# Raw down weights in two buffers loaded a unit ahead, and two steps of the operand and weight preparation moved

## The chip, the cores and the metric

The kernel runs on one core of a Trainium2 chip. The time is the device time of one execution in microseconds, as a median over runs. A core has TensorE (PE, matrix products), VectorE (DVE), ScalarE (ACT), GpSimd (POOL) and SyncE (SP, which here only issues DMAs); PEld is TensorE's loading of weights.

## The reference

Two branches on the same 2048 x 576 input are mixed by a gate. The second branch, a gated network with 4608 hidden columns, takes most of the time.

```python
x = A_x                                          # 1 x 2048 x 576, float32
g = _sigmoid((x * gate_w).sum(-1, keepdims=True))
a = _A_ref(x, A_wqkv, A_w_phi, A_wo)             # linear attention, 32 heads, learned feature map
b = _B_ref(x, B_W_gate, B_W_up, B_W_down)
return g * a + (1 - g) * b

def _B_ref(x, W_gate, W_up, W_down):             # 576 x 4608, 576 x 4608, 4608 x 576
    gate = jnp.einsum("bsd,df->bsf", x, W_gate)
    up = jnp.einsum("bsd,df->bsf", x, W_up)
    gate = gate * (lambda x, dt: x.astype(dt))(gate > 0, gate.dtype)
    h = gate * up
    return jnp.einsum("bsf,fd->bsd", h, W_down)
```

## The kernel before

**Arithmetic.** Each float32 operand is split into a high and a low part (`high` on ScalarE, `low` on VectorE), and a product is the sum of high x high, low x high and high x low on TensorE. Products of 2 x 2 blocks are made with seven block products in place of eight, from sums and differences of blocks (of the input `xo`, of the gate and up weights `wb`/`ws`, of the down weights `wd`).

**Order of the work.** The attention branch fills the first 340 us or so. Then come 72 *units*: units 0 to 35 do the first half of the rows for each of 36 blocks of hidden columns, units 36 to 71 the second half. A unit is seven *steps* j = 0 to 6, all written by `step(u, j)`; each engine works through its instructions in the order in which they are written (`in_order`). A step has one block product of the gate/up stage on PE (`product`, line 1140, seven matmuls; the seven operands are taken in the order `SEQ` = 1, 5, 6, 2, 7, 3, 4) and one block product of the down stage (`down`, line 1171, three matmuls, and two more for the rest columns in some steps). The down stage works on pairs of units: in an odd unit it does the second half (m = 1) of the pair before, in an even unit the first (m = 0) of the pair just made. So two units hold 14 x 7 + 14 x 3 + 8 = 148 matmuls: 78 in an even unit and 70 in an odd one.

**Down weights.** `load_down(g)` brings the raw down weights of pair g, `wdr`, 128 x 1152, into a single buffer, at step 5 of an even unit (line 918). `prepare_down` makes the operands `wd` from them in the next odd unit (m = 0) and the even one after it (m = 1): step 0 high parts of three blocks (ACT, line 1103), step 1 their low parts (DVE, 1106), step 2 four sums of blocks on GpSimd, in place in `wdr` (1092 to 1095), step 4 the high and step 5 the low parts of these. The rest columns go with m = 0 (`rest_weights`).

**At the turn**, units 35 to 37, the seven operands of the second half replace those of the first, as `swap_in` writes it: operands 1 and 5 come through `xr` (high part, line 827, and low part with its rest rows, 831 and 841), the others are loaded into `xo` and split in place (856, 857, 861), with the rest rows' low part on GpSimd (841).

**In the first half** VectorE and ScalarE also make the operands `wb` and `ws` of the unit to come, from raw weights `wr`, and store them to memory (`wbd`, `wsd`); the second half only loads these (911, 912).

**Copies that PE needs.** In step 1 ScalarE copies `cx` to `cy` (line 1379); the product of step 2 writes `cx` again. In step 5 VectorE adds `cx` into `u` (1383) before the product of step 6.

Of the kernel before, what the change touches and what calls it, by code (L numbers as in the profile page):

```python
# [7 lines left out]
F32 = mybir.dt.float32  # L8
# [7 lines left out]
P = 128  # L16
# [67 lines left out]
def gated_mix_kernel(  # L84
# [24 lines left out]
    nc = tc.nc  # L109
# [101 lines left out]
    with tc.tile_pool(name="ps_v", bufs=1, space=PSUM) as ps_v:  # L211
# [7 lines left out]
        for k in range(5):  # L219
            w = raw.tile([P, TB + VW], F32, name="xwv", tag="raw")  # L220
# [559 lines left out]
    wdrp = ctx.enter_context(tc.tile_pool(name="wdrp", bufs=1, **L_))  # L780
# [54 lines left out]
    def operand(hf, i):  # L835
        operand_high(hf, i)
        operand_low(hf, i)
# [26 lines left out]
    RAW, WO, WDR = {}, {}, {}  # L864
    units = [(0, c) for c in range(NC)] + [(1, (c - 2) % NC) for c in range(NC)]
# [46 lines left out]
        nc.sync.dma_start(o.bitcast(F32), wsd[c])  # L912
        WO[u] = {1: (b, 0), 2: (b, 1), 4: (b, 2), 5: (o, 2), 6: (o, 0), 7: (o, 3), 3: (o, 1)}

    def load_down(g):
        if g < 2 * NG:
            WDR[g] = wdrp.tile([P, 9 * P], F32, name="wdr")
            nc.sync.dma_start(WDR[g], wd[units[2 * g][1] // 2])

    def low_parts(f, u):  # L920
        f(u, low_w)
# [79 lines left out]
    with in_order(tc, nc, nc.tensor, nc.vector, nc.scalar, nc.gpsimd, nc.sync):  # L1001
        project_out(2, 1)
        for k in (2, 1, 0):
            quotient(3, k)
        for k in (2, 1, 0):
            operand_rows(3, k)
        whole(x1)
        RS.close()
        pad = ctx.enter_context(tc.tile_pool(name="pad2", bufs=1, **R_))
        pad.tile([P, 24], F32, name="pad2")  # L1010
        xo2 = ctx.enter_context(tc.tile_pool(name="xo2", bufs=4, **R_))
        wop = ctx.enter_context(tc.tile_pool(name="wop", bufs=2, **R_))
        wraw = ctx.enter_context(tc.tile_pool(name="wraw", bufs=2, **R_))
        load_w(0)
        load_w(1)
        for i in range(3, 7):
            load_in_place(0, i)
        load_rests(0, (3, 4, 5))
        load_down(0)
        project_out(2, 2)  # L1020
        blocks(0, high_w)
        low_parts(blocks, 0)
        project_out(2, 3)
        project_out(2, 4)
        blocks(1, high_w)
        sums_of_blocks(0)
        operand_high(0, 2)
        project_out(3, 0)
        block_sums(0, high_w)
        low_parts(blocks, 1)  # L1030
        operand_low(0, 2)
        load_rests(0, (6,))
        load_w(2)
        low_parts(block_sums, 0)
        high_in_place(0, 3)
        project_out(3, 1)
        low_of_place(3)
        sums_of_blocks(1)
        high_in_place(0, 4)
        project_out(3, 2)  # L1040
        high_in_place(0, 5)
        low_of_place(4)
        project_out(3, 3)
        block_sums(1, high_w)
        low_parts(block_sums, 1)
        low_of_place(5)
        project_out(3, 4)
# [18 lines left out]
    WD, W4, HID, ACC, ACC4, BANK, REST = {}, {}, {}, {}, {}, {}, {}  # L1066
# [6 lines left out]


    def down_raw(g, m):
        return WDR[g][:, m * 4 * P:(m + 1) * 4 * P].rearrange("p (b q) -> p b q", b=4)

    def down_tile():
        return wdp.tile([P, 18 * P], F32R, name="wd")
# [27 lines left out]

    def rest_weights(g, step):

        a = WDR[g][:, 8 * P:].rearrange("p (c q) -> p c q", c=2)  # L1110
        if step == 0:
            nc.scalar.activation(W4[g][:, 0:2, 0], a, AF.Copy)
        elif step == 1:
            tt(out=W4[g][:, 0:2, 1], in0=a, in1=W4[g][:, 0:2, 0].bitcast(F32), op=SUB)  # L1114
            pt(out=a[:, 0], in0=a[:, 0], in1=a[:, 1], op=ADD)  # L1115
        elif step == 2:
            nc.scalar.activation(W4[g][:, 2, 0], a[:, 0], AF.Copy)
            nc.scalar.activation(W4[g][:, 3], W4[g][:, 1].bitcast(F32), AF.Copy, scale=-1.0)
        else:
            tt(out=W4[g][:, 2, 1], in0=a[:, 0], in1=W4[g][:, 2, 0].bitcast(F32), op=SUB)  # L1120

    def plain_down(g, f):

        if f is high:
            o = down_tile()
            WD[g] = o[:, :16 * P].rearrange("p (s q) -> p s q", s=2)
            W4[g] = o[:, 16 * P:].rearrange("p (b s q) -> p b s q", b=2, s=2)
        f(WD[g], WDR[g][:, :8 * P])
        f(W4[g].rearrange("p b s q -> p s b q"), WDR[g][:, 8 * P:].rearrange("p (b q) -> p b q", b=2))

# [157 lines left out]
    def swap_in(u, j):  # L1290

        i = j + 7 * (u - NC + 1)
        if 2 <= i < 7:
            if i in (2, 3):
                load_rests(1, (2, 3, 4) if i == 2 else (5, 6))
            load_in_place(1, i)
        if i in (1, 2):
            operand(1, i - 1)
        if 2 <= i - 5 < 7:
            low_in_place(1, i - 5)  # L1300
        if 2 <= i - 4 < 7:
            high_in_place(1, i - 4)
        if 2 <= i - 5 < 7:
            low_rest(1, i - 5, pt)
# [48 lines left out]
    def prepare_down(g, m, j):  # L1353

        if j == 0:
            down_blocks(g, m, high)
        elif j == 1:
            down_blocks(g, m, low)
        elif j == 2:
            down_sums_of_blocks(g, m)  # L1360
        elif j == 4:
            down_block_sums(g, m, high)
        elif j == 5:
            down_block_sums(g, m, low)
        if m == 0 and j in (0, 1, 4, 5):
            rest_weights(g, (0, 1, 4, 5).index(j))

    def step(u, j):


        g, odd = divmod(u, 2)
        v, q = u + 1, g - 1
# [16 lines left out]
        old = not odd and g > 0  # L1389

        if j == 0:
            if u > 0:
                a = gate_last(*LATE.pop())
# [85 lines left out]
        elif j == 6:  # L1479
            a = T["g2"]  # L1480
# [5 lines left out]
            w = WO.pop(u)  # L1486
# [11 lines left out]
            prepare_down(g, 0, j)  # L1498
        elif old:
            prepare_down(q, 1, j)  # L1500
        if old and j == 5:
            load_down(g)
        if old and j == 6:
            ODD.pop(q)
        if g > 0:
            s = 7 * odd + j
# [35 lines left out]
    with in_order(tc, nc, nc.tensor, nc.vector, nc.scalar, nc.gpsimd, nc.sync):  # L1542
# [4 lines left out]
        g = 2 * NG - 1  # L1547
# [86 lines left out]
def _layout(A_x, A_wqkv, A_w_phi, A_wo, B_W_gate, B_W_up, B_W_down, gate_w):  # L1634
    import numpy as np

    xT = np.ascontiguousarray(_by_tiles(A_x[0].T).swapaxes(0, 1))
    xs = np.ascontiguousarray(_by_halves(A_x[0].T).transpose(2, 0, 1, 3))
    wqT = _by_groups(np.concatenate([A_wqkv[:, :D].T, A_wqkv[512:, :D].T], axis=1))
    wkT = _by_groups(np.concatenate([A_wqkv[:, D:2 * D].T, A_wqkv[512:, D:2 * D].T], axis=1))  # L1640
    v = np.zeros((D, VW), A_wqkv.dtype)
    v[:, 0] = gate_w
    for j in range(NQ):
        n = NV[j]
        v[:, j * GS + 1:j * GS + 1 + n] = A_wqkv[:, 2 * D + QG * j:2 * D + QG * j + n]
    wv = np.ascontiguousarray(_by_tiles(v).swapaxes(0, 1))
    phi = np.zeros((FG, NF, FG), A_w_phi.dtype)
    for h in range(H):
        j, i = divmod(h, FH)
        phi[i * DH:(i + 1) * DH, j, i * DH:(i + 1) * DH] = A_w_phi[h]  # L1650
    wo = np.concatenate([A_wo, A_wo[:, 512:]], axis=1)
    wo_rows = [r for k in range(4)
               for r in (*range(G * k, G * k + QG),
                         *range(4 * G + k // 2 * QG + k % 2 * 20, 4 * G + k // 2 * QG + k % 2 * 20 + 20),
                         *range(G * k + QG, G * k + G))]
    wo_rows += [*range(4 * G + 40, 4 * G + QG), *range(5 * G - 14, D)] * 2
    wo = np.ascontiguousarray(wo[wo_rows].reshape(5, P, 5, P).transpose(2, 1, 0, 3))
    g, u = (_by_halves(w).reshape(2, 3, P, NC, P) for w in (B_W_gate, B_W_up))
    wgu = np.stack([g[0], g[1], u[1], u[0]])
    wgu = np.ascontiguousarray(wgu.transpose(3, 2, 0, 1, 4))  # L1660
    d = B_W_down.reshape(NC // 2, 2, P, D)
    halves = d[..., :512].reshape(NC // 2, 2, P, 2, 2, P)
    blocks = [halves[:, 0, :, 0], halves[:, 1, :, 0], halves[:, 1, :, 1], halves[:, 0, :, 1]]
    blocks = np.stack(blocks, axis=2).transpose(0, 1, 3, 2, 4).reshape(NC // 2, P, 8 * P)
    wd = np.ascontiguousarray(np.concatenate([blocks, d[:, 0, :, 512:], d[:, 1, :, 512:]], axis=2))
    ident = np.eye(P, dtype=np.float32)
    mask = np.zeros((QK, QG + 4), np.float32)
    spread = np.zeros((4, H, 5, P), np.float32)
    copies = spread[:2]
    for r in range(QK):  # L1670
        h = r // (2 * DH)
        mask[r, h * DH:(h + 1) * DH] = 1.0
        mask[r, QG + h] = 1.0
        mask[r, QG + 3] = 1e-6 if r % (2 * DH) < DH else 0.0
    for k in range(5):
        for r in range(P):
            copies[:, wo_rows[k * P + r] // DH, k, r] = 1.0
    spread = spread.reshape(4 * H, 5, P)
    return {"xT": xT, "xs": xs, "wqT": wqT, "wkT": wkT, "wv": wv, "phi": phi, "wo": wo, "wgu": wgu,
            "wd": wd, "ident": ident, "mask": mask,  # L1680
            "spread": spread}
# [16 lines left out]
```

## Time and profile before

| | |
|---|---|
| runs | 1574.77, 1574.79, 1572.11 us; median 1574.77 |
| profiled execution | 1575.22 us, of it the span of the trace 1573.5 |
| PE busy | 1553.8 us, 99% of the span, 7715 matmuls |
| DVE, ACT, POOL busy | 1249.5 (79%), 800.8 (51%), 272.9 us (17%) |
| TensorE clock granted, mean | 0.998 |
| DMA | 283.43 MB, 180 GB/s in the mean |

PE's busy time is a modelled one: a matmul shows some 391 ns, while the next begins well before that has passed, so the pace is read from how many matmuls lie in a stretch. A few records of matmuls can be missing. A wait is shown as engine and line, the tile's name, and behind the arrow what came last. "SPq" is the queue in which SP issues DMAs. Idle time of an engine costs something only where PE comes to wait for it.

### The profile page before, as it was taken

Reading aid. Unit: us, or ns where it says so; the run is one execution under the profiler, and the core shown is the slowest. Engines: PE = TensorE matmul, PEld = TensorE weight load, DVE = VectorE, ACT = ScalarE, POOL = GpSimd, SP = SyncE. Lnnn points to the kernel's source line nnn. Section 1 sums busy time; section 2 is a strip of 40 time slices with the busy share of each in tenths; the row PEclk is TensorE's granted clock in tenths of the full one; section 3 lists DMA queues with packets and bytes.
Section 4 is the critical chain, followed back from the end, with each engine's and each line's share of the span. In section 5 each row is a group of like instructions: output and inputs, shape, how many; then the busy total and the mean of one; then the engine's idle time right before and its main releaser. Section 6 shows DMA issues by size and latency. Waiting matters only on the chain.

```text
span 1573.5 us, 20844 instructions
## 1 busy us (share of the span) xinstructions
PE 1553.8 (99%) x7715; PEld 1294.8 (82%) x7715; DVE 1249.5 (79%) x1964; ACT 800.8 (51%) x1408; POOL 272.9 (17%) x405
## 2 busy tenths in 40 slices
PE   9999999999999999999999998999999999999998
PEld 9999996687887888877888886888888888888886
DVE  4997776499999989998988988767667777667776
ACT  4354335566777767767777775332333332332332
POOL 0126522112111112111111113111111111111110
PEclk9999999999999999999999999999999999999999
DMA  5355405596755585565455424643443433433432
GB/s 165 105 197 188 174 27 150 184 359 270 265 200 201 216 286 206 217 224 212 175 214 224 187 96 161 223 153 137 182 152 132 181 141 147 186 138 135 188 133 75
DMA packets 64545, 283.43 MB, mean 180 GB/s; under 512 B 6802, under 2 KB 17298, under 8 KB 55740
## 3 DMA queue, kind: packets, MB, share of 16 engines
q1 hardware_dynamic: 61228, 270.34, 47.0%
q0 software_dynamic: 2352, 10.11, 1.9%
q10 hardware_dynamic: 864, 1.65, 0.3%
q8 instruction: 61, 1.00, 0.3%
q14 instruction: 40, 0.33, 0.1%
HBM read 172.07 MB, written 108.60 MB: 178 GB/s over the span
## 4 chain that ended last, share of the span: by engine, by line
PE 78%; DVE 15%; DMA 4%; ACT 1%; issue 1%; POOL 0%; SPq 0%; ACTq 0%; DVEq 0%; POOLq 0%
PE cx L1140 23%; PE pd L1171 16%; PE ca L1140 11%; PE cy L1140 6%; PE kv L175 4%; PE pk L175 3%; PE pq L175 3%; DMA wdr<-wd 3%; PE pm L1171 3%; DVE hl L1276 2%; DVE ac L1237 2%; DVE ws L877 1%; DVE g L1325 1%; PE kv L421 1%; DVE wd L1106 1%
## 5 line engine op out<-in xcount | busy, mean ns | idle before, releaser
L1171 PE MATMUL pd<-hh,wd 128*128 128x512 f32 x980 | 383.2, 391 | 0.1
L1186 DVE TENSOR_TENSOR ac<-pd,ac 128x512 f32<-128x512 f32 x238 | 164.5, 691 | 139.6 <-PE pd L1171 139.5
L1140 PE MATMUL cx<-xo,ws 128*128 128x512 f32 x1008 | 254.6, 392 | 10.0 <-ACT cy L1379 7.8
L1140 PE MATMUL cx<-xo,wb 128*128 128x512 f32 x1008 | 252.8, 391 | 0.7 <-DVE u L1383 0.7
L1140 PE MATMUL ca<-xo,ws 128*128 128x512 f32 x1008 | 252.8, 391 | 0.0
L1271 ACT ACTIVATE hh<-g 128x512 fp32r<-128x512 f32 x249 | 148.3, 623 | 201.0 <-DVE g L1325 183.6
L1140 PEld LDWEIGHTS cx<-xo,ws 128*128 128x128 f32 x1008 | 188.0, 188 | 54.9 <-ACT cy L1379 14.1
L1140 PEld LDWEIGHTS cx<-xo,wb 128*128 128x128 f32 x1008 | 188.6, 188 | 42.1 <-DVE u L1383 2.7
L1140 PEld LDWEIGHTS ca<-xo,ws 128*128 128x128 f32 x1008 | 189.9, 188 | 39.7 <-DVE xo L861 0.4
L1171 PEld LDWEIGHTS pd<-hh,wd 128*128 128x128 f32 x980 | 184.6, 188 | 39.2 <-ACT pd L1220 0.8
L1171 PE MATMUL pd<-hl,wd 128*128 128x512 f32 x490 | 191.6, 391 | 0.0
L1276 DVE TENSOR_TENSOR hl<-g,hh 128x512 fp32r<-128x512 f32 x249 | 173.0, 695 | 0.2 <-ACT hh L1271 0.2
L1103 ACT ACTIVATE wd<-wdr 128x384 fp32r<-128x384 f32 (+2 forms) x142 | 80.9, 570 | 161.7 <-DMA wdr<-wd 134.8
L1140 PE MATMUL cy<-xo,wb 128*128 128x512 f32 x504 | 126.7, 391 | 0.0
L1092 POOL TENSOR_TENSOR wdr<-wdr 128x128 f32<-128x128 f32 x70 | 33.5, 478 | 472.5 <-DVE wd L1106 472.5
L1140 PEld LDWEIGHTS cy<-xo,wb 128*128 128x128 f32 x504 | 95.3, 189 | 19.9
L1171 PEld LDWEIGHTS pd<-hl,wd 128*128 128x128 f32 x490 | 92.2, 188 | 19.7 <-DVE hl L1276 0.7
L1106 DVE TENSOR_TENSOR wd<-wdr,wd 128x384 fp32r<-128x384 f32 (+2 forms) x142 | 88.2, 622 | 23.7 <-ACT wd L1103 23.1
L1325 DVE TENSOR_TENSOR g<-g,g 128x512 f32<-128x512 f32 x140 | 97.5, 697 | 2.4
L1115 POOL TENSOR_TENSOR wdr<-wdr 128x64 f32<-128x64 f32 x35 | 11.5, 329 | 502.2 <-DVE wd L1114 493.4
L1237 DVE TENSOR_TENSOR ac<-pd,ac 128x512 f32<-128x512 f32 x114 | 78.1, 685 | 6.9 <-PE pd L1171 5.8
L1340 ACT ACTIVATE g<-cx 128x512 f32<-128x512 f32 x73 | 43.5, 596 | 78.5 <-PE cx L1140 77.5
(259 smaller groups left out, 2721.2 us busy)
## 6 DMA issues: line engine op xcount, KB each, us to landing
wsd<-ws SPq DMA_DIRECT2D x34, 1280.0 KB
ws<-wsd SPq DMA_DIRECT2D x34, 1280.0 KB
wbd<-wb SPq DMA_DIRECT2D x34, 960.0 KB
wb<-wbd SPq DMA_DIRECT2D x34, 960.0 KB
wr<-wgu SPq DMA_DIRECT2D x36, 768.0 KB
wdr<-wd SPq DMA_DIRECT2D x36, 576.0 KB
eT<-et SPq DMA_DIRECT2D x10, 594.0 KB
xt<-xb SPq DMA_DIRECT2D x7, 768.0 KB
```

The source lines that it names most:

```text
L175: nc.tensor.matmul(ps, w, m, start=i == 0, stop=i == len(pairs) - 1)
L1092: pt(out=a[:, 2], in0=a[:, 2], in1=a[:, 3], op=ADD)
L1103: nc.scalar.activation(o[:, 0], a, AF.Copy)
L1106: tt(out=o[:, 1], in0=a, in1=o[:, 0].bitcast(F32), op=SUB)
L1140: nc.tensor.matmul(ps, w, v, start=first and m == 0, stop=m == len(pairs) - 1, skip_group_check=True)
L1171: mm = lambda ps, w, v, a, z: nc.tensor.matmul(ps, w, v, start=a, stop=z, skip_group_check=True)
L1186: tt(out=a, in0=ps, in1=a, op=ADD)
L1237: tt(out=a, in0=ps, in1=a, op=ADD)
L1271: nc.scalar.activation(h, src, AF.Copy)
L1276: tt(out=l, in0=src, in1=h.bitcast(F32), op=SUB)
L1325: tt(out=b, in0=a, in1=b, op=SUB)
L1340: nc.scalar.activation(a, ps, AF.Copy)
```

## The change

It has three parts, and a layout that goes with them.

1. The raw down weights of a pair lie in two buffers, `wdr0` (128 x 640: the first four blocks and the rest columns) and `wdr1` (128 x 512: the other four). Part 0 is loaded at step 0 of an even unit and read from step 0 of the odd unit after it; part 1 is loaded at step 0 of an odd unit and read from step 0 of the next even one.
2. At the turn, operand 1's high part stays in step 1 of unit 35, and its low part goes to step 2; operand 5's high part goes to step 3 and its low part to step 4. Before, both parts were made in one step, 1 and 2.
3. GpSimd's sums of down weight blocks are written at step 3, not at step 2.

```diff
-    def load_down(g):
+    def load_down(g, m):
         if g < 2 * NG:
-            WDR[g] = wdrp.tile([P, 9 * P], F32, name="wdr")
-            nc.sync.dma_start(WDR[g], wd[units[2 * g][1] // 2])
+            n = 5 - m
+            w = WDR[g, m] = wdrp.tile([P, n * P], F32, name=f"wdr{m}")
+            nc.sync.dma_start(w, wd[units[2 * g][1] // 2, :, 5 * P * m:5 * P * m + n * P])
...
-        load_down(0)
+        load_down(0, 0)
+        load_down(0, 1)
...
     def down_raw(g, m):
-        return WDR[g][:, m * 4 * P:(m + 1) * 4 * P].rearrange("p (b q) -> p b q", b=4)
+        return WDR[g, m][:, :4 * P].rearrange("p (b q) -> p b q", b=4)
...
-        if i in (1, 2):
-            operand(1, i - 1)
+        if i in (2, 4):
+            operand_low(1, i // 2 - 1)
+        if i in (1, 3):
+            operand_high(1, i // 2)
...
-        elif j == 2:
+        elif j == 3:
             down_sums_of_blocks(g, m)
...
-        if old and j == 5:
-            load_down(g)
+        if old and j == 0:
+            load_down(g, 0)
+        if odd and j == 0 and g > 0:
+            load_down(g, 1)
```

`rest_weights` and `plain_down` read the same blocks from the two buffers (the last pair's high and low parts are made in two instructions in place of one), and the host lays the blocks out in the new order. The lines below 918 move down by one to seven.

How the instructions move is shown at three places.

*SP in the first half.* An even and an odd unit, before: `wr` are the raw gate and up weights for the unit after next, `wbd` and `wsd` the stores of steps 2 and 5.

```order
L870 DMA wr_6630<-wgu 128x1536
L1448 DMA wbd_68<-wb_6628 128x1920
L1456 DMA wsd_69<-ws_6708 128x2560
L918 DMA wdr_6749<-wd 128x1152
L328 DMA xt_66<-xb_5701 128x3x256
L870 DMA wr_6787<-wgu 128x1536
L1448 DMA wbd_68<-wb_6785 128x1920
```

And after, an odd and an even unit:

```order
L870 DMA wr_5893<-wgu 128x1536
L919 DMA wdr1_5898<-wd 128x512
L1453 DMA wbd_68<-wb_5891 128x1920
L1461 DMA wsd_69<-ws_5958 128x2560
L328 DMA xt_66<-xb_5715 128x3x256
L870 DMA wr_6041<-wgu 128x1536
L919 DMA wdr0_6045<-wd 128x640
L1453 DMA wbd_68<-wb_6039 128x1920
```

One load behind the stores of the even unit has become one in each unit, behind the load of `wr` and ahead of the stores.

*VectorE in unit 35.* `pd` is the down stage's sum, 831 and 841 are the low parts of operands 1 and 5. Before:

```order
L1114 TENSOR_TENSOR wd_8879<-wdr_8845,wd_8879 128x2x64
L831 TENSOR_TENSOR xo_8908<-xr_8710,xo_8908 128x1024
L841 TENSOR_TENSOR xo_8908<-xr_8710,xo_8908 32x512
L1237 TENSOR_TENSOR ac_3683<-pd0_8904,ac_3683 128x512
L831 TENSOR_TENSOR xo_8935<-xr_8712,xo_8935 128x1024
L841 TENSOR_TENSOR xo_8935<-xr_8712,xo_8935 32x512
L1276 TENSOR_TENSOR hl_8899<-g1_8824,hh_8898 128x512
```

After:

```order
L1116 TENSOR_TENSOR wd_8913<-wdr0_8766,wd_8913 128x2x64
L1240 TENSOR_TENSOR ac_3685<-pd0_8940,ac_3685 128x512
L831 TENSOR_TENSOR xo_8944<-xr_8744,xo_8944 128x1024
L841 TENSOR_TENSOR xo_8944<-xr_8744,xo_8944 32x512
L1279 TENSOR_TENSOR hl_8935<-g1_8860,hh_8934 128x512
L1330 TENSOR_TENSOR g1_8860<-g2_8830,g1_8860 128x512
L1240 TENSOR_TENSOR ac_3683<-pd0_8940,ac_3683 128x512
L831 TENSOR_TENSOR xo_8991<-xr_8746,xo_8991 128x1024
```

The addition of `pd` now stands ahead of operand 1's low part, and three instructions between that and operand 5's.

*GpSimd in unit 36, and SP behind it.* The rest rows of operands 6, 2, 7, 3 and 4 (841) and the four sums, before:

```order
L841 TENSOR_TENSOR xo_8933<-xr_8929,xo_8933 32x512
L841 TENSOR_TENSOR xo_8957<-xr_8929,xo_8957 32x512
L1092 TENSOR_TENSOR wdr_8845<-wdr_8845 128x128
L1093 TENSOR_TENSOR wdr_8845<-wdr_8845 128x128
L1094 TENSOR_TENSOR wdr_8845<-wdr_8845 128x128
L1095 TENSOR_TENSOR wdr_8845<-wdr_8845 128x128
L841 TENSOR_TENSOR xo_8981<-xr_8929,xo_8981 32x512
L841 TENSOR_TENSOR xo_8998<-xr_8954,xo_8998 32x512
```

After:

```order
L841 TENSOR_TENSOR xo_8963<-xr_8959,xo_8963 32x512
L841 TENSOR_TENSOR xo_8989<-xr_8959,xo_8989 32x512
L841 TENSOR_TENSOR xo_9015<-xr_8959,xo_9015 32x512
L1094 TENSOR_TENSOR wdr1_8916<-wdr1_8916 128x128
L1095 TENSOR_TENSOR wdr1_8916<-wdr1_8916 128x128
L1096 TENSOR_TENSOR wdr1_8916<-wdr1_8916 128x128
L1097 TENSOR_TENSOR wdr1_8916<-wdr1_8916 128x128
L841 TENSOR_TENSOR xo_9034<-xr_8986,xo_9034 32x512
```

Operand 7's rest rows now come before the sums. SP in the same units, the load for unit 37 first before and then after:

```order
L1247 DMA outT<-ac_3682 128x512
L918 DMA wdr_9155<-wd 128x1152
L1247 DMA outT<-ac_3680 128x512
L1148 DMA ac_3680<-att_64 128x512
L1247 DMA outT<-ac_3682 128x512
```
```order
L846 DMA xo_9052<-xt_66 128x1024
L919 DMA wdr0_9072<-wd 128x640
L1250 DMA outT<-ac_3682 128x512
L1250 DMA outT<-ac_3684 128x512
L1250 DMA outT<-ac_3682 128x512
```

The load has moved from between the stores of the outputs to just behind the last operand's load.

More of the change, by code (lines that the diff above doesn't have):

```diff
@@ L1108, in rest_weights @@
     def rest_weights(g, step):
-        a = WDR[g][:, 8 * P:].rearrange("p (c q) -> p c q", c=2)
+        a = WDR[g, 0][:, 4 * P:].rearrange("p (c q) -> p c q", c=2)
         if step == 0:
@@ L1127, in plain_down @@
             W4[g] = o[:, 16 * P:].rearrange("p (b s q) -> p b s q", b=2, s=2)
-        f(WD[g], WDR[g][:, :8 * P])
-        f(W4[g].rearrange("p b s q -> p s b q"), WDR[g][:, 8 * P:].rearrange("p (b q) -> p b q", b=2))
+        for m in range(2):
+            f(WD[g][:, :, 4 * P * m:4 * P * (m + 1)], WDR[g, m][:, :4 * P])
+        f(W4[g].rearrange("p b s q -> p s b q"), WDR[g, 0][:, 4 * P:].rearrange("p (b q) -> p b q", b=2))
     def product(ps, u, n, first):
@@ L1664, in _layout @@
     blocks = np.stack(blocks, axis=2).transpose(0, 1, 3, 2, 4).reshape(NC // 2, P, 8 * P)
-    wd = np.ascontiguousarray(np.concatenate([blocks, d[:, 0, :, 512:], d[:, 1, :, 512:]], axis=2))
+    wd = np.ascontiguousarray(np.concatenate([blocks[:, :, :4 * P], d[:, 0, :, 512:], d[:, 1, :, 512:], blocks[:, :, 4 * P:]], axis=2))
     ident = np.eye(P, dtype=np.float32)
```

## The prediction

> **What bounds the kernel now.** I read the engine totals first, then busy time by stretches, then who waited for whom, then the order of time at the few places where TensorE stood.
>
> ```profile
> PE 1553.8 (99%) x7715; PEld 1294.8 (82%) x7715; DVE 1249.5 (79%) x1964; ACT 800.8 (51%) x1408; POOL 272.9 (17%) x405
> ```
> ```profile
> core 0: us, PE busy (x) PEld busy (x) DVE busy (x) ACT busy (x) POOL busy (x), PEclk, DMA share, GB/s
> 600.00:650.00 50.00, 50.00 (x221) 41.05 (x220) 47.89 (x75) 37.52 (x64) 8.09 (x13) 1.00 0.53 200
> 650.00:700.00 50.00, 48.52 (x212) 39.19 (x212) 45.08 (x69) 34.95 (x61) 8.11 (x14) 1.00 0.63 233
> 1000.00:1050.00 50.00, 50.00 (x223) 41.42 (x222) 34.14 (x58) 16.27 (x33) 6.51 (x14) 1.00 0.43 162
> 942.32:964.69 22.37, 20.11 (x79) 15.20 (x78) 22.34 (x27) 14.03 (x24) 11.89 (x9) 0.92 0.26 95
> 964.69:984.65 19.96, 17.79 (x71) 14.22 (x70) 14.14 (x24) 8.12 (x17) 2.57 (x5) 0.91 0.71 258
> ```
>
> TensorE is the bound; 221 matmuls in 50 us is its full pace, and a stretch with 212 has lost about 2 us. So only time in which PE stands or runs slowly can be won. The last two rows are units 36 and 37, the turn from the first half of the sequence to the second: the clock column falls below 1.00 only there.
>
> How much is lost outside the turn is read off one repeating event, the issue of the raw down weights, once in two units:
>
> ```profile
> 377.63 0.33 SPq L918 DMA_DIRECT2D wdr<-wd  x1
> 923.56 0.33 SPq L918 DMA_DIRECT2D wdr<-wd  x1
> 999.02 0.33 SPq L918 DMA_DIRECT2D wdr<-wd  x1
> 1535.76 0.33 SPq L918 DMA_DIRECT2D wdr<-wd  x1
> ```
>
> There are 16 periods between the first two rows and 16 between the last two. The second half takes (1535.76 - 999.02) / 16 = 33.55 us for two units, the first half (923.56 - 377.63) / 16 = 34.12 us. The code gives both the same 148 matmuls (14 products of 7, 14 down products of 3, 8 for the rest columns), so the undisturbed matmul is 0.2267 us, and the first half loses 16 x 0.57 = 9.2 us. What ends the waits:
>
> ```profile
> ACT wd L1103 <- DMA wdr<-wd: 134.8, 29, 8.5
> PE cx L1140 <- ACT cy L1379: 7.8, 9, 2.2
> PE cx L1140 <- POOL xo L841: 1.9, 1, 1.9
> SPq L911 <- PE cx L1140: 278.2, 32, 15.4
> ```
>
> The first is large but is ScalarE's idleness; PE feels it only through the second, as one odd unit shows:
>
> ```profile
> 446.13 0.33 SPq L918 DMA_DIRECT2D wdr<-wd  x1
> 451.60 0.53 ACT L1103 ACTIVATE wd<-wdr 128x384 fp32r<-128x384 f32 x1 [2.38 <-DMA wdr<-wd]
> 452.23 0.58 ACT L1379 ACTIVATE cy<-cx 128x512 f32<-128x512 f32 x1
> 452.87 1.89 PE L1140 MATMUL cx<-xo,ws 128*128 128x512 f32 x7 [0.35 <-ACT cy L1379]
> ```
>
> The load is issued at step 5 of an even unit, its first reader comes two steps later, and behind that reader in ScalarE's order stands the copy cy<-cx that product 6 needs.
>
> **The change, part by part.** (a) *Two buffers, loaded a unit ahead.* Each part is now issued at step 0, behind the load of the gate and up weights, about 16 us before its first reader, where 5.5 us (446.13 to 451.60) is what it takes now. What stands before it in the queue is, by the shapes, a 1280 KB store and a 768 KB load; with itself (320 or 256 KB) 2.4 MB. At 200 GB/s for a DMA share of 0.53 the engines would move 377 GB/s when full: an estimate of 6.4 us. So the wait goes, with ten us to spare. Its 35 more DMA issues cost SP 0.33 us each, in a queue that waits anyway. The buffer is free: its last reader is the low part at step 5 of the unit before. Nothing that PE needs queues behind it before the stores at steps 2 and 5. Value between 5.6 and 9.2 us: the upper end is the whole excess, the lower counts only the stops behind cy, 7.8 us less the 2.17 us of unit 37 (below). I take 9.2, since a stop also costs a slow restart (seven matmuls in 1.89 us at 452.87), and since the second half shows what the same matmuls cost without loss.
>
> In the second half ScalarE's waits vanish too and PE gains nothing: 223 matmuls in 50 us already. The last raw load still waits for the low part in unit 70, as the row at 1535.76 does, so the tail neither gains nor loses.
>
> (b) *Unit 37.* Here the load was issued late, at step 5 of unit 36 and behind two output stores:
>
> ```profile
> 968.96 0.52 ACT L1103 ACTIVATE wd<-wdr 128x384 fp32r<-128x384 f32 x1 [6.60 <-DMA wdr<-wd]
> 970.93 0.58 ACT L1379 ACTIVATE cy<-cx 128x512 f32<-128x512 f32 x1
> 971.56 2.23 PE L1140 MATMUL cx<-xo,ws 128*128 128x512 f32 x7 [2.17 <-ACT cy L1379]
> 973.58 0.63 PE L1171 MATMUL pd<-hh,wd 128*128 128x512 f32 x1
> ```
>
> The unit took 19.96 us for 70 matmuls that need 15.87: 4.1 us, the 2.17 us stop and then matmuls at a lower clock (0.91 over the unit). The load now stands ahead of the stores. I take 4.1; the low end is 2.2, if a late VectorE brings a stop of its own and the lower clock stays.
>
> (c) *Unit 36: GpSimd's sums and the operands' low parts.* Three engines, in one place:
>
> ```profile
> 948.85 1.31 POOL L1092 TENSOR_TENSOR wdr<-wdr 128x128 f32<-128x128 f32 x1 [1.26 <-DVE wd L1106]
> 951.65 1.32 POOL L1095 TENSOR_TENSOR wdr<-wdr 128x128 f32<-128x128 f32 x1
> 953.05 4.64 POOL L841 TENSOR_TENSOR xo<-xr,xo 32x512 fp32r<-32x512 f32 x3
> 954.36 2.07 PE L1140 MATMUL cx<-xo,ws 128*128 128x512 f32 x7 [1.90 <-POOL xo L841]
> 956.23 0.63 PE L1171 MATMUL pd<-hh,wd 128*128 128x512 f32 x1
> 956.65 0.76 PE L1171 MATMUL pd<-hl,wd 128*128 128x512 f32 x1
> 961.86 1.86 PE L1140 MATMUL cx<-xo,wb 128*128 128x512 f32 x7 [0.36 <-DVE u L1383]
> 954.78 1.78 DVE L1276 TENSOR_TENSOR hl<-g,hh 128x512 fp32r<-128x512 f32 x1
> 956.48 2.29 DVE L861 TENSOR_TENSOR xo<-xo 128x1024 fp32r<-128x1024 f32 x1
> 961.03 0.68 DVE L1383 TENSOR_TENSOR u<-cx,u 128x512 f32<-128x512 f32 x1
> ```
>
> The four sums hold GpSimd from 948.85 to 952.97, and the low rows for operand 7 come after them: 1.90 us of PE. After the change those rows go first and the sums sit where they bother nobody for another step. But the unit's 4.7 us (22.37 against 78 x 0.2267 = 17.68) do not come back with that. At 961.86, even after the stop and the slow stretch, PE waits for VectorE's L1383: VectorE was the last to be ready. It is 22.34 of 22.37 us busy, with operations stretched to 1.78 and 2.29 us while GpSimd works. GpSimd's amount is unchanged, so I expect VectorE to finish this unit as late as before, except for its lead from unit 35:
>
> ```profile
> 927.30 0.53 ACT L1103 ACTIVATE wd<-wdr 128x384 fp32r<-128x384 f32 x1 [1.24 <-DMA wdr<-wd]
> 930.02 0.39 PE L1171 MATMUL pd<-hh,wd 128*128 128x512 f32 x1
> 930.12 1.47 ACT L827 ACTIVATE xo<-xr 128x1536 fp32r<-128x1536 f32 x1
> 931.62 1.23 DVE L831 TENSOR_TENSOR xo<-xr,xo 128x1024 fp32r<-128x1024 f32 x1 [3.00 <-ACT xo L827]
> 932.86 0.68 DVE L841 TENSOR_TENSOR xo<-xr,xo 32x512 fp32r<-32x512 f32 x1
> 933.58 0.69 DVE L1237 TENSOR_TENSOR ac<-pd,ac 128x512 f32<-128x512 f32 x1
> ```
>
> VectorE stood 3.00 us for the high part. Moved a step, the low part has L1237 in front of it, whose matmul ends at 930.41: it fills that hole until 931.1, L831 and L841 follow to 933.0, and the group that ended at 934.27 ends 1.2 us sooner. VectorE has no pause from there to unit 36, so I carry 1.2 us. Bounds: -0.6 (the lead, less a slow-clock stretch that falls where VectorE doesn't hide it, 1.8) and 4.7 (all of the unit).
>
> That 1.8 is a clock of 0.92 over 22.37 us: 3.6 us at half pace (0.42 us from one matmul to the next at 956.23, not 0.2267), half of them lost, behind a stop of 1.90 us. The Trainium skill, "TensorE: Matmul & The Clock Gate", section "HAM oscillation — how this bites in real kernels", gives as its rule that idle gaps up to about 3.4 us are safe. By that rule a new stop of 2 us in unit 36 costs only itself and the sum stays as below; by the rows a stop of 1.90 us was enough, and the time would be 1.8 us longer.
>
> The sum: 9.2 + 4.1 + 1.2 = 14.5 us off the profiled execution, 1575.22 (span 1573.5 and 1.7 around it), gives 1560.7. The median of the runs shown, 1574.77, is 0.45 lower, which is less than the 2.7 us between those runs; I forecast 1560.5.
>
> **Rivals.**
> - *The turn clears fully.* If VectorE is less stretched once GpSimd's order is changed, all 4.7 us of unit 36 return: 3.5 more, 1557.0. Against it: the row at 961.86.
> - *Slow clock again.* PE stops about 2 us in unit 36, now for operand 3's low part, and the half pace follows: 1562.3.
> - *VectorE becomes the first half's bound.* It is busy 47.89 of 50 us in the stretch at 600 us. If half of the returned 9.2 us comes back as its waits: 1565.1. Against it: in that very stretch PE lost nothing.
> - *The load still lands late.* The two parts wait behind the large store and load. If that takes over 16 us, (a) is void: 1569.7. The estimate of 6.4 us speaks against it.
> - *Slower.* In the second half the raw loads now travel with the 2240 KB of operands each unit. If they make those land x us after their unit's start in each of 34 units, the time is 1560.5 + 34x: slower from x = 0.42, and 1580.9 at 0.6. Against it: SP sits 278.2 us in 32 waits (8.7 each) before these loads, and the DMA share there is 0.43.
>
> **How the numbers follow.** Chances: forecast 0.58, the turn clears 0.12, slow clock 0.10, VectorE 0.12, late landing 0.04, slower 0.04. The forecast's own range is 1558.5 to 1562.5. For 8 in 10 I take it from the clear turn to just past the VectorE case: 1556.5 to 1566.0. A change of 0.2% (3.1 us) is about what measurement tells from none. All cases but the last two are far below 1571.6, and the late landing lies below it but near: faster 0.93, same 0.03, slower 0.04.
>
> **What would show it.** (a): no wait of ACT wd for wdr in the first half, and raw loads, now one a unit, 33.5 to 33.7 us apart in pairs. (b): unit 37 at 15.9 to 16.5 us, clock 1.00. (c): no PE wait for POOL xo; a wait of the products for operand 3 or for u on VectorE instead; unit 36 at 20 to 22 us. I am wrong if PE still idles behind cy in odd units, or if PE's pace falls below 220 matmuls in 50 us in the second half.

## The result, and the profile after

The changed kernel takes 1561.53 us (median of four runs, 1561.34 to 1562.32) where the kernel before takes 1574.68: a ratio of 0.9921, 95% interval 0.9904 to 0.9939. The profiled execution took 1562.32 us, its span 1560.5. The forecast was 1560.5, in a range of 1556.5 to 1566.0.

The page's first line after, then busy time by stretches (the last two rows are units 36 and 37 again):

```profile
PE 1547.9 (99%) x7715; PEld 1294.2 (83%) x7715; DVE 1246.6 (80%) x1965; ACT 803.4 (51%) x1409; POOL 265.1 (17%) x405
```
```profile
core 0: us, PE busy (x) PEld busy (x) DVE busy (x) ACT busy (x) POOL busy (x), PEclk, DMA share, GB/s
600.00:650.00 50.00, 50.00 (x221) 41.06 (x221) 47.57 (x73) 37.58 (x64) 7.67 (x13) 1.00 0.55 205
650.00:700.00 50.00, 50.00 (x222) 41.25 (x221) 46.86 (x75) 35.49 (x62) 7.33 (x14) 1.00 0.62 234
1000.00:1050.00 50.00, 50.00 (x222) 41.42 (x221) 37.17 (x61) 17.31 (x34) 6.64 (x13) 1.00 0.41 157
932.10:955.54 23.44, 20.43 (x79) 15.39 (x78) 23.36 (x28) 14.20 (x24) 10.99 (x9) 0.93 0.36 128
955.54:971.41 15.87, 15.87 (x71) 13.14 (x70) 13.55 (x23) 8.09 (x17) 2.46 (x5) 1.00 0.83 283
```

The stretch from 650 us, which had 212 matmuls, has 222. Unit 37 takes just the 15.87 us that its 70 matmuls need. Unit 36 has become longer: 23.44 us, and was 22.37.

Who waited for whom, after:

```profile
PE pd L1174 <- DVE hl L1279: 2.1, 2, 1.9
PE ca L1143 <- DVE xo L861: 0.8, 1, 0.8
PE cx L1143 <- ACT cy L1384: 0.5, 2, 0.3
ACT wd L1105 <- PE pm L1174: 114.0, 17, 7.0
SPq L911 <- PE cx L1143: 485.5, 32, 15.9
```

ScalarE's 134.8 us of waiting for the raw down weights are gone, and with them PE's stops behind `cy` (7.8 us became 0.5); PE's wait for GpSimd's rest rows (`xo`, 1.9 us) is gone too. Most of what is left in the units is PE waiting for VectorE, at the turn. SP now waits 485.5 us ahead of the second half's operand loads (278.2 before), and PE waits for none of them. The loads of part 0, by SP's queue:

```profile
393.09 0.33 SPq L919 DMA_DIRECT2D wdr<-wd  x1
426.62 0.33 SPq L919 DMA_DIRECT2D wdr<-wd  x1
897.19 17.22 SPq L919 DMA_DIRECT2D wdr<-wd  x2
```

Two units lie between the first two rows, 33.5 us; thirty between the first and the third, 15 periods of 33.6 us. Before, a period was 34.12 us. Each of these loads goes off 1.4 us before the even unit begins, some 20 us before ScalarE reads it in the odd one.

By the start of each unit's first product, the 12.9 us between the two spans (1573.45 and 1560.53) lie so:

| part | before to after, us | gain |
|---|---|---|
| up to unit 3 (attention, first units) | 379.36 to 378.57 | 0.79 |
| lost in units 3 to 34, beyond 0.2267 us a matmul | 9.61 to 0.90 | 8.71 |
| lost in unit 35 | 0.74 to 0.00 | 0.74 |
| unit 36 | 22.37 to 23.45 | -1.08 |
| unit 37 | 19.96 to 15.87 | 4.09 |
| units 38 to 70 | 554.43 to 554.43 | 0.00 |
| from unit 71 on | 34.37 to 34.69 | -0.32 |

The first row has nothing to do with the change: in the thirteen profiled executions of this case that time was between 376.7 and 380.5 us whatever had been edited. It is why medians below that differ by 2 us or less are read from the units, not from the totals.

### The profile page after: what moved, and what is told of

Read it like the earlier page. It is cut to its first block, busy times and chain, and to the rows that moved or that the text cites. A ratio compares the mean times of both kernels' runs of the same rounds, so it can differ in the third digit from the quotient of the medians.

```text
span 1560.5 us, 21012 instructions
## 1 busy us (share of the span) xinstructions
PE 1547.9 (99%) x7715; PEld 1294.2 (83%) x7715; DVE 1246.6 (80%) x1965; ACT 803.4 (51%) x1409; POOL 265.1 (17%) x405
## 3 DMA queue, kind: packets, MB, share of 16 engines
q10 hardware_dynamic: 864, 1.65, 0.3%
## 4 chain that ended last, share of the span: by engine, by line
PE 94%; DVE 3%; DMA 1%; ACT 1%; issue 0%; POOL 0%; SPq 0%; DVEq 0%; POOLq 0%; ACTq 0%
PE cx L1143 28%; PE pd L1174 21%; PE ca L1143 14%; PE cy L1143 7%; PE kv L175 4%; PE pm L1174 4%; PE pk L175 3%; PE pq L175 3%; PE kv L421 1%; PE po L562 1%; PE pv L237 1%; PE ptr L379 1%; PE pw L175 1%; PE psf L259 1%; PE pw L657 1%
## 5 line engine op out<-in xcount | busy, mean ns | idle before, releaser
L1105 ACT ACTIVATE wd<-wdr 128x384 fp32r<-128x384 f32 (+1 forms) x143 | 80.7, 566 | 114.0 <-PE pm L1174 114.0
L1240 DVE TENSOR_TENSOR ac<-pd,ac 128x512 f32<-128x512 f32 x114 | 78.1, 685 | 22.6 <-PE pd L1174 21.4
L1108 DVE TENSOR_TENSOR wd<-wdr,wd 128x384 fp32r<-128x384 f32 (+1 forms) x143 | 88.2, 618 | 2.1 <-ACT wd L1105 1.0
```

The lines of the kernel that those rows point to most:

```text
L1105: nc.scalar.activation(o[:, 0], a, AF.Copy)
L1108: tt(out=o[:, 1], in0=a, in1=o[:, 0].bitcast(F32), op=SUB)
L1240: tt(out=a, in0=ps, in1=a, op=ADD)
```

## Experiments

"Lost" is what PE lost in units 3 to 34; the ideal length of unit 36 is 17.68 us, of unit 37 15.87. Ratios are against the kernel before, run on the same chip.

| kernel | median, us | ratio (95%) | lost, units 3-34 | unit 36 | unit 37 |
|---|---|---|---|---|---|
| before | 1574.68 | 1 | 9.61 | 22.37 | 19.96 |
| after | 1561.53 | 0.9921 (0.9904-0.9939) | 0.90 | 23.45 | 15.87 |
| e1 buffers only | 1560.29 | 0.9917 (0.9901-0.9934) | 0.90 | 22.07 | 15.87 |
| e2 moves only | 1573.1 | 0.9995 (0.9986-1.0005) | 8.90 | 23.57 | 18.41 |
| e3 sums back | 1561.12 | 0.9928 (0.9913-0.9943) | 0.91 | 23.03 | 15.87 |
| e4 operands back | 1560.66 | 0.9924 (0.9909-0.9939) | 0.86 | 22.55 | 15.87 |
| e5 no rest rows (one run) | 1558.34 | - | 0.88 | 19.20 | 15.87 |
| e6 rest rows on VectorE | 1562.54 | 0.9929 (0.9914-0.9944) | 0.82 | 23.35 | 15.87 |
| e7 two rest rows on VectorE | 1561.95 | 0.9926 (0.9911-0.9941) | 0.92 | 22.99 | 15.87 |
| e8 both loads at step 5 | 1563.41 | 0.9936 (0.9920-0.9953) | 2.18 | 23.71 | 15.87 |
| e9 e1, totals early | 1560.37 | 0.9917 (0.9900-0.9934) | 0.83 | 21.97 | 15.87 |
| e10 after, totals early | 1559.39 | 0.9913 (0.9898-0.9927) | 0.89 | 21.75 | 15.87 |

### Which part of the change brings it: e1 to e4

e1 keeps the buffers, with the loads a unit ahead, and undoes both moves; e2 keeps the moves and undoes the buffers and the early loads; e3 and e4 undo one move each.

```diff
 e1 and e4 (operands), from after; e2 has the reverse, from before
-        if i in (2, 4):
-            operand_low(1, i // 2 - 1)
-        if i in (1, 3):
-            operand_high(1, i // 2)
+        if i in (1, 2):
+            operand(1, i - 1)
 e1 and e3 (sums), from after; e2 has the reverse, from before
-        elif j == 3:
+        elif j == 2:
             down_sums_of_blocks(g, m)
```

e2 keeps the single buffer `wdr` and its load at step 5 as they were before.

> The changed kernel with its two moves undone (operands 1 and 5 split in one step each, sums at step 2); only the two buffers and the early loads stay. Theory T (the whole gain is the loads': 9.5 us in the first half and 4.1 us in unit 37; unit 36 is set by VectorE, whatever GpSimd's order): within 1 us of the changed kernel's 1561.5, unit 36 between 22 and 23.5 us, in it a PE stop on GpSimd's rest rows of 1 to 2 us. Rival M (the moves carry a part of the gain): 1563.5 or more.

> The kernel before with the two moves alone, raw weights in one buffer and loaded late. Theory T: 1574 to 1576, nothing won; unit 36 at about 23 us as in the changed kernel, unit 37 again near 20 us, the first half at 34.1 us for two units. Rival M: 1572 or less.

> The changed kernel with GpSimd's sums back at step 2. Theory T: within 1 us of 1561.5 either way; PE's stop on GpSimd's rest rows comes back in unit 36 (1 to 2 us) and the stop on VectorE's hl (1.91 us) shrinks by as much. Rival M: 1563.5 or more, the rest-row stop is added.

> The changed kernel with operands 1 and 5 each split in one step again. Theory T: within 0.7 us of 1561.5; VectorE waits 2 to 3 us for ScalarE's high part in unit 35 and PE loses up to 0.7 us in unit 35. Rival M: 1562.5 or more, since VectorE enters unit 36 over 1 us later and unit 36 grows by that.

e1 has the whole gain and e2 none that can be measured: the buffers, with their early loads, carry it. In e2 the waits are those of before:

```profile
ACT wd L1103 <- DMA wdr<-wd: 136.6, 30, 8.3
PE cx L1140 <- ACT cy L1381: 7.8, 11, 2.2
```

With the buffers in, unit 36 is shortest without the moves (22.07), and longest with both (23.45). One profile stands behind each of these lengths; e11, which runs the instructions of after up to unit 40, took 23.71 us for its unit 36, so a difference of 0.3 us says nothing. What PE stopped for there, in e1, e3 and e4 (one row each; in the last two the half pace follows, as the seven matmuls in 3.22 us and the single one of 0.79 us show):

```profile
946.32 1.89 PE L1143 MATMUL cx<-xo,ws 128*128 128x512 f32 x7 [1.61 <-POOL xo L841]
```
```profile
942.98 3.22 PE L1143 MATMUL cx<-xo,ws 128*128 128x512 f32 x7 [2.32 <-POOL xo L841]
```
```profile
945.77 0.79 PE L1174 MATMUL pd<-hl,wd 128*128 128x512 f32 x1 [2.19 <-DVE hl L1279]
```

Where the sums stand at step 2 (e1, e3), PE stops for GpSimd's rest rows; where they stand at step 3 (e4, after), it stops for VectorE's `hl`, about as long (1.6 and 2.3 us, 2.2 and 1.9). The stop changes its cause and gets no shorter. In unit 35 e1 and e4 lose 0.55 us, after and e3 nothing; with that, units 35 and 36 lose 4.9 us in e1, 5.4 in e3 and in e4, 5.8 in after.

### What holds VectorE up in unit 36: e5 to e7

```diff
 e5: the low part of five operands' rest rows is left out
-            low_rest(1, i - 5, pt)
+            XR.pop((1, i - 5))
 e6: GpSimd (pt) gives them to VectorE (tt); e7: only the last two of the five
+            low_rest(1, i - 5, tt)
```

> The changed kernel without the low part of the five rest rows that GpSimd makes in unit 36 (left out: those rows keep their high part's value). Theory L (VectorE's two-input operations and GpSimd's keep each other out, and that is what makes unit 36 long): VectorE's hl and xo operations there fall from 1.75 and 2.30 us to 0.7 and 1.2, and unit 36 falls from 23.4 to 19 to 20.5 us. Rival B (VectorE simply has too much to do there): operations as long as elsewhere were never the cause, unit 36 stays above 22.

> The changed kernel with those five rest rows on VectorE (0.68 us each) in place of GpSimd. Theory L: 3.0 to 3.4 us more work for VectorE, 3.5 to 4 us less blocking: unit 36 between 21.5 and 23.5 us, time within 1.5 us of 1561. Rival B: 3 us more work, unit 36 at 26 us, 1564.

> The changed kernel with only the last two rest rows (operands 3 and 4) on VectorE. Theory L: the two long operations, 1.75 and 2.30 us, fall to 0.7 and 1.2 for 1.2 us more work: unit 36 about 1 us shorter, 22 to 22.8 us. Rival B: 1.2 us longer, 24.6.

Unit 36 in e5 and in e6, by engine:

```profile
932.44:951.64 19.20, 18.35 (x80) 14.41 (x78) 19.17 (x27) 14.09 (x24) 3.96 (x4) 1.00 0.43 155
```
```profile
932.19:955.54 23.35, 19.16 (x80) 14.22 (x78) 23.00 (x32) 14.20 (x24) 3.41 (x4) 1.00 0.36 129
```

Without GpSimd's five operations the unit falls from 23.45 to 19.20 us, and VectorE is still busy for all of it (19.17). So VectorE has 19.2 us of work, with GpSimd's four sums (3.96 us) still beside it, in a unit for which PE needs 17.68, and the five rest rows add some 4 us, though VectorE does none of them. The groups of VectorE's operations in that unit show how, of after and then of e5 (columns: busy us, mean ns of one, idle before):

```profile
L861 DVE TENSOR_TENSOR xo<-xo 128x1024 fp32r<-128x1024 f32 x5 | 7.4, 1483 | 0.0
L1279 DVE TENSOR_TENSOR hl<-g,hh 128x512 fp32r<-128x512 f32 x5 | 5.8, 1169 | 0.0
L1240 DVE TENSOR_TENSOR ac<-pd,ac 128x512 f32<-128x512 f32 x7 | 4.8, 679 | 0.0
```
```profile
L861 DVE TENSOR_TENSOR xo<-xo 128x1024 fp32r<-128x1024 f32 x5 | 6.3, 1268 | 0.0
L1240 DVE TENSOR_TENSOR ac<-pd,ac 128x512 f32<-128x512 f32 x6 | 4.1, 680 | 0.0
L1279 DVE TENSOR_TENSOR hl<-g,hh 128x512 fp32r<-128x512 f32 x5 | 3.6, 720 | 0.0
```

The same operation takes 1169 ns beside GpSimd's rest rows and 720 without them; L1240, which has one operand in PSUM (`pd`), takes 679 and 680. The Trainium skill, "SBUF — State Buffer", section "SBUF: two separate sides", says that VectorE with two SBUF inputs and GpSimd lock each other out for a whole instruction; these rows agree. In e6, VectorE does the five itself at 710 ns and the unit is as long (23.35): lending them to GpSimd costs VectorE in waiting what it saves in work. e7, with two of the five moved, took 22.99 us, a little under both; 22 to 22.8 was expected.

### Late, held by the buffer, or too large: e8

Both new buffers, but the loads of both parts at step 5 of the even unit, as before.

```diff
-        if old and j == 0:
+        if old and j == 5:
             load_down(g, 0)
-        if odd and j == 0 and g > 0:
             load_down(g, 1)
```

> The changed kernel with both raw loads issued at step 5 of the even unit, as the one load was before: two buffers, but no lead for part 0. If the lead is what brought the gain (theory T), ScalarE waits for wdr again in odd units, by 0.5 to 2 us less than before since part 0 is 320 of 576 KB; the first half loses 3 to 8 us and unit 37 1 to 4 us: 1564 to 1572. If the split into two buffers brought it (rival S): 1560 to 1562.

7.4 of the 8.7 us of the first half come back without any load a unit ahead (9.61 to 2.18), and all of unit 37's 4.09. Neither expectation holds: if the lead were all, 3 to 8 us would be lost in the first half and 1 to 4 in unit 37; if the split were all, the time would be 1560 to 1562, and it is 1563.41.

But e8 differs from before in two things: part 0 has a buffer that was read out a unit earlier, and its load is 320 KB where the one load was 576. Which of the two counts is seen by when the data moved. In the first half, unit 7 of e8 (the same rows of before are those at 446.13 and 451.60 in the prediction):

```profile
442.09 1.81 SPq L919 DMA_DIRECT2D wdr<-wd  x2
448.21 0.53 ACT L1105 ACTIVATE wd<-wdr 128x384 fp32r<-128x384 f32 x1 [1.56 <-DMA wdr<-wd]
```

From issue to reading it is 6.1 us, and was 5.5, though the load is smaller. Means of the 15 odd units from 5 to 33, by the DMA packets in the two traces, in us from the start of the odd unit:

| | before | e8 |
|---|---|---|
| load of `wdr` (e8: of part 0) issued | -1.90 | -3.34 |
| last packet of the store of `ws` ahead of it starts | 0.07 | 0.68 |
| first packet of the load starts | 0.42 | 1.02 |
| last packet of the load ends | 3.17 | 2.30 |
| ScalarE's first reading | 3.60 | 2.81 |

The issue comes 1.4 us earlier and the data 0.6 us later: in both kernels they come 0.3 us behind the last packet of the store. The reading is earlier because part 0 takes 1.28 us to move and the whole took 2.75. So in the first half the free buffer only lets the load wait longer behind the store, and what e8 wins there it wins by the smaller first part. No run has a smaller first load without the second buffer, which would show it directly.

At the turn it is otherwise. SP's wait for the load in before, over the whole run; SP and VectorE of before in unit 36; SP of e8 there:

```profile
SPq L918 <- DVE wd L1106: 282.7, 35, 28.8
```
```profile
959.40 3.27 SPq L1247 DMA_DIRECT2D outT<-ac  x2
962.83 0.68 DVE L1106 TENSOR_TENSOR wd<-wdr,wd 128x512 fp32r<-128x512 f32 x1
963.54 0.34 SPq L918 DMA_DIRECT2D wdr<-wd  x1
```
```profile
950.78 3.27 SPq L1250 DMA_DIRECT2D outT<-ac  x2
954.15 1.10 SPq L919 DMA_DIRECT2D wdr<-wd  x2
```

Before, 35 of 36 loads waited for the low part that VectorE makes from the one buffer. At the turn the load goes off 0.87 us behind the two output stores and 0.03 us after VectorE's last reading of the one buffer, which stands at the end of VectorE's backlog, 1.15 us before unit 36 ends. In e8 part 0 goes off right behind the stores, 2.4 us before the end (unit 37 starts at 956.56). Its first packet starts 1.1 us earlier against unit 37 than before, and it moves in 2.03 us where the whole took 3.40. ScalarE's wait is 2.86 us where it was 6.60; PE does not stop. So in unit 37 the free buffer and the smaller part both count, and no run separates them. The load a unit ahead adds the last 1.3 us of the first half: ScalarE still waits 24.4 us for `wdr` in e8, in 16 places, and in after it doesn't.

### Room for VectorE: e9 and e10

The last pair's running totals are added into the accumulators in unit 35, where VectorE stands for 3 to 4 us, with four additions; two additions of unit 36 (`L1245`) go. e9 is so made from e1, e10 from after.

```diff
+        if u == 2 * NG - 1 and j < 2:
+            for a, n in ((ACC[0, 0, 0, 1], 6), (TOTAL[0, 7], 6)) if j == 0 else ((ACC[0, 1, 0, 1], 7), (ACC[0, 1, 0, 0], 7)):
+                tt(out=a, in0=a, in1=TOTAL[0, n], op=ADD)
...
-        more = (m, {1: 6, 6: 7}.get(n))
+        more = (m, {1: 6, 6: 7}.get(n) if m else None)
```

> Buffers alone, without the two moves, and in it the last pair's running totals are added into the accumulators in unit 35 (four VectorE additions where VectorE stands 4.2 us) and not between the products of unit 36 (two additions less there). Theory V (unit 36 is as long as VectorE's own queue): two operations of 0.60 us less, so unit 36 is 1.2 us shorter than the 22.07 us of buffers alone, about 20.9 us, and unit 35 is unchanged; total 1559. Rival S (the stops in unit 36 are set by which operand is late, not by the sum of VectorE's work): unit 36 stays at 22.0 us.

> The changed kernel with the same edit: four additions into unit 35, two out of unit 36. Theory V: unit 36 falls by 1.2 us from 23.45 us to about 22.2 us, and the low operand parts that the moves put there keep it longer than the same edit does on buffers alone. Rival S: unit 36 stays near 23.4 us. A third outcome, below 20.9 us, would say that the moves do pay once VectorE has room.

In e9 unit 36 is 0.1 us shorter, in e10 1.7. Both theories are half right: which engine sets the end depends on where the sums stand. PE in e9, then unit 36 of e10:

```profile
944.42 1.89 PE L1143 MATMUL cx<-xo,ws 128*128 128x512 f32 x7 [1.52 <-POOL xo L841]
```
```profile
932.04:953.79 21.75, 19.68 (x79) 14.10 (x78) 21.71 (x25) 14.20 (x24) 11.69 (x9) 1.00 0.37 136
```

In e9 GpSimd, with the four sums ahead of three rest rows, is as late as in e1, and VectorE's room is no use. In e10 the sums are out of the way of operand 3's rest rows, and the room counts: PE's one long stop has become four of 0.4 to 0.6 us, and the clock stays at 1.00. How much of the 1.7 us is VectorE's 1.2 us and how much the half pace that doesn't come, one profile does not tell; e2, with the order of after in this unit and no half pace in it, took 23.57, which speaks for VectorE. With that room the moves no longer cost anything: units 35 and 36 lose 4.1 us in e10, 4.8 in e9. e10 has the lowest median of the kernels that do the whole computation, 1559.39; its interval overlaps those of after and e1, so that it beats them is shown by units 35 and 36 of one profile each, not by the totals.

### The clock: e11

After, with 3 to 7 operations more on VectorE in 15 units of the second half, to make PE stop.

```diff
         elif j == 5:
+            if 40 <= u < 70 and u % 2 == 0:
+                for _ in range(3 + u // 2 % 5):
+                    tt(out=T["u2"], in0=T["u2"], in1=T["u2"], op=ALU.max)
```

> The changed kernel, with 3 to 7 added VectorE operations (each the maximum of u with itself, which leaves u as it is, 0.60 us each) ahead of the addition into u in step 5 of the 15 even units from 40 to 68, where PE loses nothing otherwise: so 15 stops of PE of some 1 to 4 us, one in 33.6 us. Theory H (the clock is granted by windows of 3.413 us on a fixed grid: where PE is busy for under half of a window, 1.71 us, the next window runs at half pace): the half-pace stretches are 3.41 us long, start a whole number of 3.413 us from each other, and follow just those windows that hold less than 1.71 us of PE's work, whatever the length of the stop; stops of 1.7 to 3.4 us are followed by one or not by where they fall on the grid, stops under 1.7 us never. Rival G (only a stop of over 3.4 us brings the half pace): none but the longest are followed by one. Rival L (the length of the stop alone decides, from about 1.9 us): one length splits the stops.

One run, 1582.06 us. Nine stops came, not 15 (the shorter additions hid, or cost under 0.3 us): three each of 0.70, 1.43 and 2.15 us. Half pace followed two of the three of 2.15 us and none of the others. The stretches began at 949.08 (the turn), 1160.70 and 1334.78 us: 62 and 113 times 3.413 us after the first. On that grid, one stop that was followed and one that was not:

```profile
1157.29:1160.70 3.41, 1.26 (x6) 0.97 (x6) 3.27 (x6) 0.00 (x0) 0.00 (x0) 1.00 0.00 0
1160.70:1164.11 3.41, 3.41 (x10) 2.66 (x9) 3.32 (x6) 0.00 (x0) 0.00 (x0) 0.50 0.29 74
1505.45:1508.87 3.42, 1.55 (x7) 0.94 (x5) 3.21 (x5) 0.00 (x0) 0.00 (x0) 1.00 0.00 0
1508.87:1512.28 3.41, 3.13 (x14) 2.59 (x15) 3.38 (x7) 0.07 (x1) 0.00 (x0) 1.00 0.17 27
```

The rivals fall: a stop of under 3.4 us is enough, and the same 2.15 us brings the half pace or not. The grid holds. The limit of 1.71 us that was expected does not: a window with 1.55 us of PE's work was not followed.

## Why the prediction came out as it did

**(a), the first half: right, 9.2 expected, 8.71 measured.** Its size is the excess over the second half's pace, and this was nearly all won: no wait of `wd` for `wdr`, pairs 33.5 to 33.6 us apart. The 0.9 us left are no stops but slightly slow starts of single matmuls, 0.1 us in about every second pair. The reason given stands: before, the load is issued too near its reader, and its data begin to move only 0.42 us into the reader's unit, behind the 1280 KB store. What the prediction missed is that the lead is not the only remedy: e8, with the load in its old place, wins 7.4 of the 8.7 us, by the smaller first part. Two numbers were off without weight: the lead is some 20 us, not 16, and the added DMA issues are 36, not 35.

**(b), unit 37: right, 4.1 expected, 4.09 measured.** The prediction blamed the place behind two output stores. That is a part of it: the load also waited 0.87 us more for VectorE's reading of the one buffer, and 576 KB took 3.40 us to move. e8 leaves the load behind the stores, and PE does not stop.

**(c), unit 36: wrong in sign.** 1.2 us shorter was expected and 1.08 longer measured, outside the bound of -0.6. The step that failed is "except for its lead from unit 35": the lead was counted on the clock, and not against PE. VectorE in unit 35 of after, with its first operation for unit 36, and the same operation before:

```profile
920.97 0.69 DVE L1240 TENSOR_TENSOR ac<-pd,ac 128x512 f32<-128x512 f32 x1 [3.19 <-PE pd L1174]
921.95 1.23 DVE L831 TENSOR_TENSOR xo<-xr,xo 128x1024 fp32r<-128x1024 f32 x1 [0.29 <-ACT xo L827]
925.50 0.69 DVE L1240 TENSOR_TENSOR ac<-pd,ac 128x512 f32<-128x512 f32 x1 [0.17 <-PE pd L1174]
932.03 0.69 DVE L1330 TENSOR_TENSOR g<-g,g 128x512 f32<-128x512 f32 x1
```
```profile
942.04 0.69 DVE L1325 TENSOR_TENSOR g<-g,g 128x512 f32<-128x512 f32 x1
```

L1240 does fill the hole, 4.7 us into the unit, as expected. But VectorE, now ahead, waits 0.29 us for ScalarE's high part and 0.17 us for PE, and comes out 0.5 us earlier in the unit (15.80 against 16.32 us after its start), not 1.2. PE regained 0.74 us in that unit. So against PE's start of unit 36 (932.10, and 942.32 before) VectorE's lead fell from 0.28 to 0.07 us: there was nothing to carry over.

Second, the bound of -0.6 supposed that VectorE's work in the unit would be stretched as before. GpSimd's rest rows stand differently between VectorE's operations now, and stretch others. GpSimd, VectorE and PE of after, at the stop:

```profile
944.81 3.28 POOL L841 TENSOR_TENSOR xo<-xr,xo 32x512 fp32r<-32x512 f32 x2
945.20 1.75 DVE L1279 TENSOR_TENSOR hl<-g,hh 128x512 fp32r<-128x512 f32 x1
946.87 2.30 DVE L861 TENSOR_TENSOR xo<-xo 128x1024 fp32r<-128x1024 f32 x1
947.00 0.50 PE L1174 MATMUL pd<-hl,wd 128*128 128x512 f32 x1 [1.91 <-DVE hl L1279]
949.23 2.07 PE L1143 MATMUL ca<-xo,ws 128*128 128x512 f32 x4 [0.81 <-DVE xo L861]
```

From the start of the unit to the end of that `hl`, VectorE took 14.24 us before (956.56) and 14.85 after (946.95); from there to the end of the unit it is 8.13 and 8.59. Before, it was late at the same time as GpSimd, and one stop of PE covered both. What the prediction did see: that the wait for GpSimd would become one for VectorE at operand 3 or nearby, and that GpSimd stretches VectorE's operations.

**The rivals.** The turn did not clear: 5.77 us are lost in unit 36. The first half's bound was not VectorE, and the second half lost nothing with the raw loads beside the operands. The slow clock came again: stop of 1.91 us, clock 0.93 over the unit. Its price was less than that rival's 1.8 us: e2 has the same order in unit 36, a stop of 1.68 us in the same place and no half pace, and from the matmul behind the stop to the unit's end it took 8.07 us where after took 8.54, as PE then waited 0.36 us for VectorE's `u`. That is 0.5 us, by one profile each.

That the rival's time, 1562.3, is the profiled execution's 1562.32 is chance, and so in part is the forecast's nearness. The sum, 1560.7, ended only 1.6 us under that execution because the miss of 2.3 us in (c), 0.5 in (a) and 0.3 in the tail (whose cause I did not trace) met 1.5 us that were in no term: unit 35's 0.74 and the start's 0.79.

**The rule on the clock** that was weighed, idle gaps up to about 3.4 us safe (the Trainium skill, "TensorE: Matmul & The Clock Gate", section "HAM oscillation — how this bites in real kernels"), does not hold here: stops of 1.9 to 2.3 us were followed by 3.41 us at half pace in before, after, e3, e4, e8 and e11. But the row as the prediction read it, "1.90 us was enough", is no rule either, as e11 shows.

## What to carry to other kernels

In these traces a reader waits for the whole of the load that brings its data: ScalarE reads 384 of the 1152 columns, and started 0.4 us behind the load's last packet. So a load that is split, with what is read first in a load of its own, can win much of a lead: nine tenths of (a) and (b) here (e8). What released a load's issue is only half of the answer; look also at when its data moved, since an earlier issue into a queue that is still busy with a large store won nothing by itself in the first half. A lead on a helper engine counts only against the engine that waits for it; take its first operation of the next stage minus that stage's start, before and after. Where two helper engines are late together, easing one gives the stop to the other: the four sums alone (e4) and the two additions alone (e9) won nothing to speak of, and together with the operands' move (e10) they lost least in units 35 and 36 of all that leave nothing out (4.1 us).

## What the runs showed of the hardware

Between 400 and 1520 us of the span, the half pace is granted in stretches of 3.41 us on a fixed grid of 3.413 us (in before at 955.90 and 972.96, five windows apart; in e11, 62 and 113). Over the 13 profiled executions, with the grid laid through each one's own half-pace stretches, all eight windows between 400 and 1520 us in which PE was busy 1.51 us or less, and none with 1.76 or more, were followed by half pace. Between these the three windows don't sort: 1.54 (before) and 1.65 (e7) were followed, 1.55 (e11) was not; PE's ends are modelled, so a tenth of a microsecond is not to be had. The window ahead of the stretch in after, and e2's stop of 2.23 us, which lies across two windows and stayed at full pace:

```profile
945.42:948.83 3.41, 1.42 (x5) 0.86 (x5) 3.41 (x2) 1.01 (x2) 2.67 (x2) 1.00 0.00 0
948.83:952.24 3.41, 3.01 (x7) 2.43 (x8) 3.41 (x6) 1.15 (x2) 0.00 (x0) 0.50 0.20 77
```
```profile
968.00:971.41 3.41, 1.76 (x8) 1.46 (x9) 2.34 (x5) 3.17 (x6) 2.56 (x5) 1.00 1.04 430
971.41:974.82 3.41, 3.41 (x17) 2.82 (x16) 2.49 (x4) 1.11 (x2) 0.00 (x0) 1.00 0.96 380
```

So a stop near 2 us (in e7 two shorter ones together, 0.84 and 1.11) costs itself and, by where it falls on the grid, up to 1.6 us more: in e11 the two units with a stretch of half pace behind their stop of 2.15 us took 21.61 and 21.72 us, the third 20.13. Where PE would have waited for VectorE anyway it is less, 0.5 us in unit 36 of after. That the window runs free is also what the Trainium skill states ("TensorE: Matmul & The Clock Gate", section "What's actually happening"); the runs add that it need not be idle, only less than about half busy.
